# A transformer block on one core: spare products in the opening, codes before background, and a root moved to GpSimd

## The chip, the cores and the metric

One core of a Trainium2 chip runs the whole program in one launch. The metric is the time of one execution in device microseconds, as the median of several runs. Shorter is better. "TensorE" is the matrix engine (PE in the profile), "VectorE" is DVE, "ScalarE" is ACT, "GpSimd" is POOL, and SyncE (SP) issues the DMAs.

## The reference

All inputs are bfloat16. The sequence has 2048 rows of 512 numbers.

```python
def _A_ref(x, wqkv, wo):                      # attention, 32 heads of 16
    qkv = ((x @ wqkv).reshape(B, S, 3, 32, 16)).transpose(2, 0, 3, 1, 4)
    q, k, v = qkv[0], qkv[1], qkv[2]
    scores = jnp.einsum("bhqd,bhkd->bhqk", q, k) * (16 ** -0.5)
    p = softmax(scores, axis=-1)
    o = jnp.einsum("bhqk,bhkd->bhqd", p, v)
    return o.transpose(0, 2, 1, 3).reshape(B, S, 512) @ wo

def _B_ref(x, w_gate, w_up, w_down):          # gated feed-forward, 1792 wide
    return (sigmoid(x @ w_gate) * (x @ w_up)) @ w_down

h  = x + _A_ref(layernorm(x), wqkv, wo)
h2 = h + _B_ref(layernorm(h), w_gate, w_up, w_down)
```

## The kernel before, in words

**Opening.** x is loaded in four chunks of 512 rows, transposed on TensorE and copied out. The first layer norm is folded into the projections: its mean is taken out of the weights, and its reciprocal deviation comes from products of x with itself (`gram`), `diagonal`, `variance`, `deviation` and `rstd0`. Keys and queries of the first four heads are built at once (`kproj0`, `queries0`, `turn_kq`). The order of these steps is not written by hand. Each is a `Task` with the engines it may run on and an assumed cost. While the program is built, a loop takes the task with the best key (start time less a share of its rank), and issues it. Products that start before the constant `COLD` are priced 1.9 times higher there. Two PSUM buffers named `g0` hold gram products, two named `h0` the key projections.

**Main stage.** The 32 heads form groups of four; a *group* of work is four heads with 512 queries, or eight heads with 256. A unit is one head strip, 128 keys and 512 score columns. 2048 units are cut into 683 *score tiles* of three. TensorE writes a tile to `pss` (L1024); two such tiles exist. ScalarE takes the exponential of all three units (128x1536) or of two (128x1024, L1375) into one of six buffers `pt`. In the second case VectorE takes the third unit: it writes a bfloat16 bit pattern that approximates the exponential (a *first code*, `J`, L1189), and when up to four first codes are together, three shifted copies of them (*codes*, L1209, kept as a `Chain`). The products of all four patterns with V are added up. TensorE's products with V go to one accumulator `acc` (L1163). When the last product of a group is in, `finish_group` transposes and normalizes it (L1105); only then may the next group's products with V begin.

Between these, TensorE works off a queue of *background*: the projections of later heads, then for each 256 rows the output projection, the second layer norm, and the feed-forward. Background is a queue of generators (`bg`); `credit` grows with every exponential and is spent by background products.

**What sets the order.** While the program is built, a planner keeps one clock per engine (`T`) and lets the engine that is furthest behind take its next step: `pe_step`, `act_step` or `dve_step`. Jobs for VectorE wait in `dq` and for ScalarE in `aq`, each with an assumed duration. `dve_step` takes the first codes before the jobs, and the jobs before the `Chain` of further codes. The engines then run the resulting queues strictly in order. `fill` adds a product without use where the planner finds TensorE too little used.

**The second layer norm.** For each of seven blocks of 256 rows, `wo_add` takes the statistics on VectorE (L162), and `newton_jobs` computes 1/sqrt(variance + 1e-5) for two columns by a bit trick and two Newton steps (L800 to L811). Two scalings (L855) need the result, then come transposes on TensorE and the feed-forward. The last block of 256 rows is done after the last exponential, by ScalarE's square root.

Of the kernel before, what the change touches and what calls it, by code (L numbers as in the profile page):

```python
# [26 lines left out]
def kernel(  # L27
# [11 lines left out]
    nc = tc.nc  # L39
    P = 128  # L40
    S, D = A_x.shape[1], A_x.shape[2]
# [9 lines left out]
    TQ = QC // P  # L51
# [55 lines left out]
    meanw = prep.tile([P, P], BF16)  # L107
# [108 lines left out]
        return ps0.tile([P, 512], FP32, name="b0")[:]  # L216

    nc.scalar.activation(out=small.tile([P, 1], FP32, name="warm")[:], in_=eps_t[:], func=ACT.Sqrt)

    kfull = small.tile([P, 1], FP32, name="kfull", bufs=1)  # L220
    buf = {}
# [221 lines left out]

    CHUNK_FIRST = (5300, 1700, -1300, 600)
    KIND_FIRST = {'g': -300, 'rc': 500, 'qm': 500, 'h': -700, 't': -700, 'rr': -2000, 'kr': 2000, 'qr': -3000, 'e': -5000, 'va': 5000, 'ke': -6000, 'va0': -6000, 'kk': -6000, 'kt': -7000}
    COLD = 7000.0
    RANKED = 0.032

    free = {"P": 0.0, "A": 2500.0, "D": 3300.0, "G": 8000.0}
    banks, grams, projs = 4, 2, 2  # L450
    left = {n for n, t in tasks.items() if t.end is None}
    while left:
        best = None
        for n in left:
            t = tasks[n]
            ends = [tasks[d].end for d in t.deps]
            if None in ends or t.bank > banks or t.gram > grams or t.proj > projs:
                continue
            at = max(ends, default=0.0) + 90
            if n == "go":  # L460
                t.end = at
                continue
            kind = n[0] if isinstance(n, tuple) else n
            rk = rank_of(n) + KIND_FIRST.get(kind, 0) + (
                CHUNK_FIRST[n[1]] if isinstance(n, tuple) else 0)
            for eng, ns, fn in t.opts:
# [12 lines left out]
        grams -= t.gram  # L479
        projs -= t.proj  # L480
        left.discard(n)
        fn()
# [14 lines left out]

    LAT = 100.0
    T = {e: max(0.0, free[e] - tasks["go"].end) for e in "PAD"}
    SPQ, LAND = 630.0, 2000.0  # L500
    sp = {"t": 0.0}

# [42 lines left out]
        def end(self):  # L545
            return None if self.job.end is None else self.job.end + self.ns

    dq, aq, chains = [], [], []
    prior = {"op": None}
    BUBBLE = 119  # L550
    class State(dict):
# [2 lines left out]
            if key == "pm":  # L554
                super().__setitem__("open", False)

    st = State(**{"n": 0, "open": False, "cur": 0, "pm": None, "mark": None, "acc": None, "mode": "b", "work": "b", "ot": 0})

    def dve(ns, fn, *deps):
        dq.append(Job(ns, fn, deps))  # L560
        return dq[-1]

    def act(ns, fn, *deps):
        aq.append(Job(ns, fn, deps))
        return aq[-1]

    class Chain:
        def __init__(self, ops, after):
            self.ops, self.after = deque(ops), after

        def left(self):
            return sum(o[0] for o in self.ops)
# [5 lines left out]
    def pending():  # L578
        return sum(c.left() for c in chains)
# [3 lines left out]

    def pop_chain():
        c = next_chain()
        T["D"] += c.cost()
        _, _, f = c.ops.popleft()
        c.after.append(object())
        prior["op"] = c.after[-1]
        f()  # L590
        if not c.ops:
            chains.remove(c)

    def flush():
        moved = True
        while moved and (dq or aq):
            moved = False
            for q, e in ((dq, "D"), (aq, "A")):
# [193 lines left out]
    def newton_jobs(dst, var, *deps):  # L792
        n = var.shape[1]
        v = small.tile([P, n], FP32, name="nv")
        y = small.tile([P, n], FP32, name="ny")
        t = small.tile([P, n], FP32, name="nt")
        V = nc.vector

        def seed():
            V.tensor_scalar(out=v[:], in0=var, scalar1=1e-5, scalar2=None, op0=ALU.add)  # L800
            V.tensor_scalar(out=t[:].bitcast(I32), in0=v[:].bitcast(I32), scalar1=1,
                            scalar2=None, op0=ALU.logical_shift_right)
            V.tensor_scalar(out=y[:].bitcast(I32), in0=t[:].bitcast(I32), scalar1=-1.0,
                            scalar2=float(0x5F3759DF), op0=ALU.mult, op1=ALU.add)

        def step(out):
            V.tensor_tensor(out=t[:], in0=y[:], in1=y[:], op=ALU.mult)
            V.tensor_tensor(out=t[:], in0=t[:], in1=v[:], op=ALU.mult)
            V.tensor_scalar(out=t[:], in0=t[:], scalar1=-0.5, scalar2=1.5,
                            op0=ALU.mult, op1=ALU.add)  # L810
            V.tensor_tensor(out=out, in0=y[:], in1=t[:], op=ALU.mult)  # L811
# [315 lines left out]
    def av_cost(uns):  # L1127
        return MM * max(sum(un.u[3] == j for un in uns) for j in range(4))
# [70 lines left out]
    def dexp_rest():  # L1199
        J, uns = half[0], half[1:]  # L1200
        half.clear()
        k = len(uns)
        j = J[:, 0:k, :]
        mine = first_codes[-1]
        mine[0] += NCODE - 1

        def code(i):
            c = dvx.tile([P, NJ, QC], U16, name="code", bufs=CB)[:, 0:k, :]
            nc.vector.tensor_scalar(out=c, in0=j, scalar1=CODE_STEP[i], scalar2=None, op0=ALU.add)  # L1209
# [7 lines left out]
        chains.append(Chain([(75 + 134 * k, 0, lambda i=i: code(i)) for i in range(NCODE)], [J]))  # L1217

    def drop_read():
        for c in (codes, first_codes):  # L1220
# [58 lines left out]
    def pe_step():  # L1279
# [109 lines left out]
    def dve_step():  # L1389
        t = T["D"]  # L1390
        job = next((j for j in dq if j.ready() is not None and j.ready() <= t), None)
        if job and jq and t - sc_end[jq[0][0]] < 400:
            dq.remove(job)
            job.place("D")
            return
        drop_read()
        if jq and sc_end[jq[0][0]] + LAT <= t + WAITJ and (half or len(first_codes) < NJB):
            n, pss, un, ex = jq.popleft()
            first = dexp_first(pss, un)
            T["D"] = max(t, sc_end[n] + LAT) + 600  # L1400
            ex_end[n] = max(un.end, T["D"])
            tc.declare_no_dep(first.ins, ex.ins, reason="other banks of the tile")
            readers[n] = (ex, first)
            return
        for job in dq:
            r = job.ready()
            if r is not None and r <= t + 60:
                dq.remove(job)
                job.place("D")
                return  # L1410
        if chains:
            pop_chain()
            return
        T["D"] = t + 40
# [19 lines left out]
            wd = load_wd()  # L1434
            load_xr(0)

    steps = {"P": pe_step, "A": act_step, "D": dve_step}
    while nxt["e"] < N or jq:
        e = nxt["e"]
        if e == N:  # L1440
            dve_step()
            continue
        steps[min("PAD", key=lambda k: T[k])]()
        if nxt["e"] > e:
            after_exp(e)
    if half:
# [107 lines left out]
```

## Time and profile before

| | before |
|---|---|
| time, median of 3 runs | 827.53 us (825.93 to 829.72) |
| the profiled execution | 828.4 us, of which the span from first to last instruction is 826.6 us |
| mean granted clock of TensorE | 0.979 |
| busy: TensorE, VectorE, ScalarE, GpSimd | 763.5, 738.2, 770.3, 8.4 us |
| first exponential starts, last one ends | 22.8 us, 794.4 us |

How to read the rows: a row of groups ends in "busy, mean ns of one | idle time of the engine just before, and what ended most of it". A row of the timeline has start, duration, engine, line, operation, output and inputs, and in brackets the idle time before it and what ended it. A row of windows has the stretch and its length, the busy time of each engine with its number of instructions, the clock granted to TensorE (1.00 is full), the share of the DMA engines, and GB/s. A row of waits has the total in us, the number of waits, and the longest.

### The profile page before, as it was taken

To read this page: it belongs to the slowest core of one execution; us is meant where nothing else is said; L and a number is where in the kernel's file an instruction comes from. 1 tells how busy PE (TensorE), PEld (TensorE's weight loads), DVE (VectorE), ACT (ScalarE), POOL (GpSimd) and SP (SyncE) were. 2 spreads that over 40 slices of the span, in tenths; PEclk is the share of its full clock that TensorE was granted. 3 is DMA by queue.
4 is the path that set the end of the run, shared out by engine and by line. 5 is a ranking of instruction groups with operands and counts; after the bars stand their busy time and mean duration, and the time that the engine had idled before them with its cause. 6 is when DMAs were issued, how large, how long until landed. Compare 5 with 4: busy or idle time off the path is not lost.

```text
span 826.6 us, 34438 instructions
## 1 busy us (share of the span) xinstructions
PE 763.5 (92%) x15176; PEld 371.3 (45%) x15179; DVE 738.2 (89%) x1410; ACT 770.3 (93%) x780; POOL 8.4 (1%) x30
## 2 busy tenths in 40 slices
PE   7899999888888998999998999999999999999998
PEld 6322222333333534455544443555454445545556
DVE  7799899999979898999999889899989998989962
ACT  6898999999998999899999998999999999999962
POOL 3000000000000000000000000000000000000000
PEclk9698999999989999999999999999999999999999
DMA  6402012122400223013101230231032202332500
GB/s 188 116 2 62 7 27 60 28 60 60 130 5 22 60 62 93 10 48 105 54 16 53 68 110 13 68 85 54 21 94 59 73 16 67 103 95 78 166 26 18
DMA packets 91860, 51.30 MB, mean 62 GB/s; under 512 B 21376, under 2 KB 90624, under 8 KB 91712
## 3 DMA queue, kind: packets, MB, share of 16 engines
q1 hardware_dynamic: 91184, 49.03, 21.5%
q8 instruction: 120, 1.97, 1.0%
q14 instruction: 28, 0.23, 0.1%
q10 hardware_dynamic: 528, 0.07, 0.1%
HBM read 39.52 MB, written 2.11 MB: 50 GB/s over the span
## 4 chain that ended last, share of the span: by engine, by line
PE 38%; ACT 37%; issue 13%; DVE 10%; DMA 1%; SPq 0%; ACTq 0%; DVEq 0%
ACT pt L1375 35%; PE pm L186 11%; PE acc L1163 11%; PE pss L1024 10%; DVE J L1189 4%; DVE code L1209 2%; PE gu L181 1%; ACT th L894 1%; DVE xs L1105 1%; DMA RQ<-rows 1%; PE hp L1519 1%; PE b L177 1%; PE g L249 1%; DVE hT L878 0%; PE pm L626 0%
## 5 line engine op out<-in xcount | busy, mean ns | idle before, releaser
L1375 ACT ACTIVATE pt<-pss 128x1024 bf16<-128x1024 f32 (+1 forms) x683 | 729.5, 1188 | 24.3 <-PE pss L1024 11.7
L1189 DVE TENSOR_SCALAR J<-pss 128x512 uint16<-128x512 f32 x480 | 320.0, 681 | 27.1 <-PE pss L1024 25.1
L1024 PE MATMUL pss<-QT,KT 32*128 32x256 bf16 (+1 forms) x3584 | 272.9, 292 | 44.6 <-ACT pt L1375 29.8
L1209 DVE TENSOR_SCALAR code<-J 128x2048 uint16<-128x2048 uint16 (+3 forms) x387 | 238.7, 645 | 0.2
L1163 PE MATMUL acc<-pt,Vaug 128*17 128x256 bf16 (+1 forms) x2742 | 222.8, 293 | 2.2 <-DVE xs L1105 1.2
L1024 PEld LDWEIGHTS <-KT 32*128 32x128 bf16 x3584 | 83.7, 92 | 249.9 <-ACT pt L1375 136.0
L1163 PE MATMUL acc<-code,Vaug 128*17 128x256 bf16 (+1 forms) x2526 | 187.7, 290 | 0.0
L1163 PEld LDWEIGHTS <-Vaug 128*17 128x17 bf16 x6110 | 137.6, 90 | 96.5 <-issue 77.0
L1163 PE MATMUL acc<-J,Vaug 128*17 128x256 bf16 (+1 forms) x842 | 136.9, 295 | 0.0
L186 PE MATMUL pm<-xT,wgu 128*32 128x256 bf16 x3136 | 117.2, 274 | 1.7 <-DVE hT L878 0.9
L186 PEld LDWEIGHTS <-wgu 128*32 128x32 bf16 x3136 | 76.7, 96 | 28.3 <-issue 25.1
L186 PE MATMUL pm<-wd,hT 128*32 128x512 bf16 x784 | 54.7, 382 | 0.4 <-DVE h L843 0.4
L878 DVE SCALAR_TENSOR_TENSOR hT<-th,pm 128x512 bf16<-128x512 f32 x49 | 33.3, 680 | 10.3 <-PE pm L186 9.3
L894 ACT ACTIVATE th<-pm 128x512 f32<-128x512 f32 x49 | 30.8, 629 | 0.8 <-PE pm L186 0.2
L1105 DVE STREAM_TRANSPOSE xs<-acc 128x512 f32<-128x512 f32 x32 | 22.8, 711 | 9.2 <-PE acc L1163 8.2
L186 PEld LDWEIGHTS <-hT 128*32 128x32 bf16 x784 | 16.1, 95 | 20.2 <-issue 12.6
L186 PE MATMUL pm<-xT,wk_sb 128*32 128x512 bf16 x256 | 19.3, 383 | 1.1 <-DVE kd L668 0.8
L186 PE MATMUL pm<-xT,wq_sb 128*32 128x512 bf16 x256 | 19.1, 382 | 0.1
L186 PE MATMUL pm<-wv_sb,xT 128*32 128x448 bf16 x256 | 17.6, 370 | 0.5 <-DVE Vaug L206 0.4
L186 PE MATMUL pm<-wo_sb,ot 128*32 128x512 bf16 x224 | 17.3, 397 | 0.7 <-DVE hT L878 0.5
L888 DVE SCALAR_TENSOR_TENSOR ob<-pm,h 128x512 bf16<-128x512 f32 x14 | 9.6, 684 | 4.9 <-PE pm L186 4.9
L1083 DVE STREAM_TRANSPOSE ot<-o 128x256 bf16<-128x256 bf16 x32 | 13.5, 432 | 0.1
(152 smaller groups left out, 344.5 us busy)
## 6 DMA issues: line engine op xcount, KB each, us to landing
wgu<-in_B_w_gate_dram SPq DMA_DIRECT2D x49, 256.0 KB
wgu<-in_B_w_up_dram SPq DMA_DIRECT2D x49, 256.0 KB
KT<-ones SPq DMA_DIRECT2D x7, 512.0 KB
out_dram<-ob SPq DMA_DIRECT2D x15, 128.0 KB
KT<-kd SPq DMA_DIRECT2D x28, 64.0 KB
QT<-qd SPq DMA_DIRECT2D x112, 16.0 KB
wd<-in_B_w_down_dram SPq DMA_DIRECT2D x1, 1792.0 KB
xr<-in_A_x_dram SPq DMA_DIRECT2D x14, 128.0 KB
```

The source lines that it names most:

```text
L177: nc.tensor.transpose(out=pt[:, b, :], in_=part, identity=ident_bf[:])
L186: nc.tensor.matmul(ps[r, :], lhsT=lhsT[:, r], rhs=rhs, start=start, stop=stop, tile_position=(0, 32 * j), skip_group_check=True)
L878: nc.vector.scalar_tensor_tensor(out=hT[:, 2 * k:2 * k + 2, :].rearrange("p f q -> p (f q)"), in0=th[:], scalar=1.0, in1=ps, op0=ALU.add, ...
L888: nc.vector.scalar_tensor_tensor(out=ob[:], in0=ps, scalar=0.5, in1=fstate.pop((h, i))[:], op0=ALU.mult, op1=ALU.add)
L894: nc.scalar.activation(out=th[:], in_=ps, func=ACT.Tanh, scale=0.5)
L1024: mm = nc.tensor.matmul(pss[:, ui, a * w:(a + 1) * w], lhsT=KT[hg[a]][32 * j:32 * j + 32, kt * P:(kt + 1) * P], rhs=(QT0[q] if q < NQC and ...
L1083: nc.vector.transpose(out=ot[:], in_=o2[:, i * NB:(i + 1) * NB, :] .rearrange("p b r -> p (b r)"))
L1105: j = st["acc"] = dve(630, lambda: nc.vector.transpose(out=xs[:].rearrange("p b r -> p (b r)"), in_=acc[:]), Mark(T["P"]))
L1163: nc.tensor.matmul(acc[32 * j:32 * j + VW, a * w:(a + 1) * w], lhsT=Vaug[:, kt, 4 * hg[a] + j, :], rhs=un.ap[:, a * w:(a + 1) * w], start= ...
L1189: first = nc.vector.tensor_scalar(out=J[:, k, :], in0=src, scalar1=128 * SC * LOG2E, scalar2=float(CODE_BASE), op0=ALU.mult, op1=ALU.add)
L1209: nc.vector.tensor_scalar(out=c, in0=j, scalar1=CODE_STEP[i], scalar2=None, op0=ALU.add)
L1375: ex = nc.scalar.activation(out=pt[:, lo:lo + wa, :], in_=pss[:, lo:lo + wa, :], func=ACT.Exp, scale=SC)
```

## The change

1. **Spare products in the opening.** 18 products of `meanw` with itself are issued at the start into a buffer `h0`. In the opening's loop, a new helper `idle` issues up to 8 products of 512 columns into a buffer `g0` where the loop sees TensorE wait; it does so in one place, between the second and the third transposition of keys. `COLD` goes from 7000 to 4500.
2. **Codes of a closed group first.** A `Chain` now knows its group. `dve_step` takes a code before the waiting jobs when the group that TensorE is closing lies more than 3 tiles back.
3. **Reciprocal root on GpSimd.** `newton_jobs` issues to GpSimd. The seed takes two instructions for three. GpSimd gets a queue `gq`, a step `gps_step` and a clock of its own in the planner. A lock between GpSimd and the chains (`lock`, `unlocked`) exists in the planner, but no job sets it.
4. **Background ahead.** When no first code waits and VectorE's clock with all its pending codes is less than 300 ns ahead of TensorE's, background may be issued with `credit` down to -4 (the third condition, fewer than 100 tiles to the group's end, always holds: a group has some 21 tiles).

```diff
+    spare = ps0h.tile([P, TQ, P], FP32, name="h0")[:]
+    for _ in range(18):
+        nc.tensor.matmul(spare[:, 0, :], lhsT=meanw[:], rhs=meanw[:], start=True, stop=True)
...
-    COLD = 7000.0
+    COLD = 4500.0
...
+    def idle(n):
+        if n > 0 and "idle" not in buf:
+            buf["idle"] = ps0g.tile([P, TQ, P], FP32, name="g0")[:]
+        for _ in range(min(n, 8)):
+            E.matmul(buf["idle"], lhsT=xT[3][:, 0, 0, :], rhs=xT[3][:, 0, :, :], start=True, stop=True)
...
         t = tasks[n]
+        if eng == "P" and free["P"] > 9000.0:
+            idle(int((start - free["P"] - 200.0) // 216))
         free[eng] = t.end = start + ns
...
+    def gps_step():
+        t = T["G"]
+        for job in gq:
+            r = job.ready()
+            if r is not None and r <= t + 60:
+                gq.remove(job)
+                job.place("G")
+                if job.lock:
+                    st["lock"] = T["G"] - job.ns, T["G"]
+                return
+        T["G"] = t + 40
...
-        V = nc.vector
+        V = nc.gpsimd
 
         def seed():
             V.tensor_scalar(out=v[:], in0=var, scalar1=1e-5, scalar2=None, op0=ALU.add)
-            V.tensor_scalar(out=t[:].bitcast(I32), in0=v[:].bitcast(I32), scalar1=1,
-                            scalar2=None, op0=ALU.logical_shift_right)
-            V.tensor_scalar(out=y[:].bitcast(I32), in0=t[:].bitcast(I32), scalar1=-1.0,
+            V.tensor_scalar(out=y[:].bitcast(I32), in0=v[:].bitcast(I32), scalar1=-0.5,
                             scalar2=float(0x5F3759DF), op0=ALU.mult, op1=ALU.add)
...
-        j = dve(600, seed, *deps)
-        j = dve(800, lambda: step(y[:]), j)
-        return dve(800, lambda: step(dst), j)
+        j = gps(1100, seed, *deps)
+        j = gps(1050, lambda: step(y[:]), j)
+        return gps(1050, lambda: step(dst), j)
...
+    HURRY = -3
...
+        group = tiles[min(e, N - 1)][-1][:2]
+        floor = -4 if not jq and T["D"] + pending() < t + 300 and lasts[group] - e < 100 else 0
         order = []
-        if st["work"] == "b" and st["mode"] != "s" and credit > 0 and not (press and pick):
+        if st["work"] == "b" and st["mode"] != "s" and credit > floor and not (press and pick):
             order.append("b")
         if last or press or good and credit < 2:
             order.append("a")
-        if credit > 0:
+        if credit > floor:
             order.append("b")
...
+        if chains and chains[0].group == gseq[st["cur"]] and lasts[chains[0].group] < nxt["e"] + HURRY:
+            pop_chain()
+            return
         for job in dq:
...
-    steps = {"P": pe_step, "A": act_step, "D": dve_step}
+    steps = {"P": pe_step, "A": act_step, "D": dve_step, "G": gps_step}
```

More of the change, by code (lines that the diff above doesn't have):

```diff
@@ L499 @@
     T = {e: max(0.0, free[e] - tasks["go"].end) for e in "PAD"}
+    T["G"] = 0.0
     SPQ, LAND = 630.0, 2000.0
@@ L546, in end @@
             return None if self.job.end is None else self.job.end + self.ns
-    dq, aq, chains = [], [], []
+    dq, aq, gq, chains = [], [], [], []
     prior = {"op": None}
@@ L555, in __setitem__ @@
                 super().__setitem__("open", False)
-    st = State(**{"n": 0, "open": False, "cur": 0, "pm": None, "mark": None, "acc": None, "mode": "b", "work": "b", "ot": 0})
+    st = State(**{"n": 0, "open": False, "cur": 0, "pm": None, "mark": None, "acc": None, "mode": "b", "work": "b", "ot": 0, "lock": (0.0, 0.0)})
     def dve(ns, fn, *deps):
@@ L565, in act, with gps, unlocked, __init__ @@
         return aq[-1]
+    def gps(ns, fn, *deps, lock=False):
+        gq.append(Job(ns, fn, deps))
+        gq[-1].lock = lock
+        return gq[-1]
+    def gps_step():
[9 more added lines that the diff above has]
+        T["G"] = t + 40
+    def unlocked(t):
+        return st["lock"][1] if st["lock"][0] <= t < st["lock"][1] else t
     class Chain:
-        def __init__(self, ops, after):
-            self.ops, self.after = deque(ops), after
+        def __init__(self, ops, after, group):
+            self.ops, self.after, self.group = deque(ops), after, group
         def left(self):
@@ L585, in pop_chain @@
         c = next_chain()
-        T["D"] += c.cost()
+        T["D"] = unlocked(T["D"]) + c.cost()
         _, _, f = c.ops.popleft()
@@ L595, in flush @@
         moved = True
-        while moved and (dq or aq):
+        while moved and (dq or aq or gq):
             moved = False
-            for q, e in ((dq, "D"), (aq, "A")):
+            for q, e in ((dq, "D"), (aq, "A"), (gq, "G")):
                 for job in list(q):
@@ L808, in step @@
             V.tensor_tensor(out=t[:], in0=t[:], in1=v[:], op=ALU.mult)
-            V.tensor_scalar(out=t[:], in0=t[:], scalar1=-0.5, scalar2=1.5,
-                            op0=ALU.mult, op1=ALU.add)
+            V.tensor_scalar(out=t[:], in0=t[:], scalar1=-0.5, scalar2=1.5, op0=ALU.mult, op1=ALU.add)
             V.tensor_tensor(out=out, in0=y[:], in1=t[:], op=ALU.mult)
-        j = dve(600, seed, *deps)
-        j = dve(800, lambda: step(y[:]), j)
-        return dve(800, lambda: step(dst), j)
+        j = gps(1100, seed, *deps)
+        j = gps(1050, lambda: step(y[:]), j)
+        return gps(1050, lambda: step(dst), j)
     out_v = out[0].rearrange("(t p) d -> p t d", p=P)
@@ L1216, in code @@
                 due[un.u[0], un.u[1], un.u[3]] -= i == NCODE - 1
-        chains.append(Chain([(75 + 134 * k, 0, lambda i=i: code(i)) for i in range(NCODE)], [J]))
+        chains.append(Chain([(75 + 134 * k, 0, lambda i=i: code(i)) for i in range(NCODE)], [J], uns[0].u[:2]))
     def drop_read():
@@ L1442 @@
             continue
-        steps[min("PAD", key=lambda k: T[k])]()
+        steps[min("PADG", key=lambda k: T[k])]()
         if nxt["e"] > e:
```

## The prediction

> **What bounds the kernel now.** I read the page first: three engines lie close together, so no share of busy time says who leads.
>
> ```profile
> PE 763.5 (92%) x15176; PEld 371.3 (45%) x15179; DVE 738.2 (89%) x1410; ACT 770.3 (93%) x780; POOL 8.4 (1%) x30
> ```
>
> Next the windows view, cut where the exponentials begin and end, and the waits and groups of their line (L1375).
>
> ```profile
> 22.84:794.42 771.58, 718.74 (x14665) 338.46 (x14668) 709.15 (x1332) 747.06 (x732) 0.30 (x1) 0.98 0.22 60
> ACT pt L1375 <- PE pss L1024: 11.7, 24, 1.0
> ACT pt L1375 <- PE acc L1163: 9.5, 4, 3.3
> L1375 ACT ACTIVATE pt<-pss 128x1024 bf16<-128x1024 f32 x481 | 469.8, 1063 | 22.6 <-PE pss L1024 11.0 <-PE acc L1163 9.5
> L1375 ACT ACTIVATE pt<-pss 128x1536 bf16<-128x1536 f32 x202 | 289.2, 1488 | 1.7 <-PE pss L1024 0.7 <-ACT pt L1375 0.3
> ```
>
> In the 771.6 us of the main stage ScalarE works 747.1 and stands still 24.5. So the time is: opening (22.8), plus ScalarE's work, plus its 24.5 us of gaps, plus the end (826.6 - 794.4 = 32.2). In the built programs the instruction order from the last score tiles to the end is the same on TensorE, ScalarE and VectorE; I take the end as unchanged. What can move is the opening, the work, and the gaps. The timeline of ScalarE names the gaps. The four long ones, each at the close of a group of heads:
>
> ```profile
> 82.15 2.37 ACT L1375 ACTIVATE pt<-pss 128x1024 bf16<-128x1024 f32 x2 [2.81 <-PE acc L1163]
> 269.89 2.85 ACT L1375 ACTIVATE pt<-pss 128x1024 bf16<-128x1024 f32 x3 [3.32 <-PE acc L1163]
> 343.59 21.43 ACT L1375 ACTIVATE pt<-pss 128x1024 bf16<-128x1024 f32 x20 [2.45 <-PE acc L1163]
> 438.94 3.71 ACT L1375 ACTIVATE pt<-pss 128x1024 bf16<-128x1024 f32 x3 [0.88 <-PE acc L1163]
> ...
> 736.87 19.78 ACT L1375 ACTIVATE pt<-pss 128x1536 bf16<-128x1536 f32 x18
> ```
>
> They make 2.81 + 3.32 + 2.45 + 0.88 = 9.46 us. (The last row, with no gap before or in it, is used below.) The second place is the first exponentials, where the granted clock (the column behind the products' count) has fallen to half:
>
> ```profile
> 25.63 2.85 ACT L1375 ACTIVATE pt<-pss 128x1024 bf16<-128x1024 f32 x3 [0.85 <-PE pss L1024]
> 28.90 1.02 ACT L1375 ACTIVATE pt<-pss 128x1024 bf16<-128x1024 f32 x1 [0.41 <-PE pss L1024]
> 30.89 1.02 ACT L1375 ACTIVATE pt<-pss 128x1024 bf16<-128x1024 f32 x1 [0.97 <-PE pss L1024]
> 32.40 1.02 ACT L1375 ACTIVATE pt<-pss 128x1024 bf16<-128x1024 f32 x1 [0.48 <-PE pss L1024]
> 33.65 7.80 ACT L1375 ACTIVATE pt<-pss 128x1536 bf16<-128x1536 f32 x7 [0.23 <-PE pss L1024]
> ...
> 19.00:20.00 1.00, 0.63 (x5) 0.71 0.03 8
> 20.00:21.00 1.00, 1.00 (x8) 0.50 0.00 0
> ...
> 33.00:34.00 1.00, 1.00 (x14) 0.96 0.47 105
> ```
>
> From the shares 0.71 and 0.96 the clock fell at 19.4 and rose at 33.1: 13.7 us at half speed, with 0.85 + 0.41 + 0.97 + 0.48 + 0.23 = 2.94 us of ScalarE's gaps. The rest of the 24.5 is small, or lies in later spells at half clock.
>
> **The opening.** In before, the first product waits for x at 3.05; four products take 0.61 us until 9 us, then 0.39:
>
> ```profile
> 0.83 0.17 DVE L132 MEMSET meanw<- 128x128 bf16 x1 [0.83 <-PEq L1538]
> 3.05 1.31 PE L177 MATMUL b<-ident_bf,code 128*128 128x128 bf16 x8 [3.05 <-DMA code<-in_A_x_dram]
> 6.67 0.61 PE L249 MATMUL g<-xT 128*128 128x128 bf16 x4
> 9.45 0.39 PE L249 MATMUL g<-xT 128*128 128x128 bf16 x4
> 6.00:7.00 1.00, 1.00 (x14) 1.00 1.01 175
> 10.00:11.00 1.00, 1.00 (x26) 1.00 0.93 300
> 19.37 0.56 PE L333 MATMUL b<-ident_bf,code 128*128 128x128 bf16 x4 [1.91 <-DVE rstd L281]
> 798.09 1.46 PE L1472 MATMUL hp<-wo_sb,ot 128*128 128x512 bf16 x6
> ```
>
> TensorE starts 14 products in the seventh microsecond and 26 in the eleventh (the column's 1.00 notwithstanding). The 18 spare products need only meanw, ready at 1.0. At 14 per us they end by 2.3, and even if they are slower the wait for x until 3.05 covers nearly all. TensorE is then busy 2 us sooner; if it speeds up 2 us sooner, 2 us of slow work shrink to 1. Bounds: +0.2 (x is late anyway and the products overhang) to -1.9; I take -1.0, between the two. The short chain from 19.4 to the first scores (transposes and the maximum product, 0.56 per four against 0.39) would run at full clock: two such steps lie on the path, -0.3. The new list order swaps a few neighbours only, and its DMAs stay in their order.
>
> The 8 products of 512 columns go ahead of the transposes that wait 1.91 us in before. Six such products take 1.46 us, so about (1.46 - 0.38) / 5 = 0.22 each beyond the first, 1.7 us for eight: the wait covers them, and without that cover they would cost 1.7. If they keep the clock up, most of the 2.94 us goes; VectorE's work and the score round trip keep some: -2.5. By the Trainium skill, "TensorE: Matmul & The Clock Gate", Part 1, the clock falls only after an idle window of about 3.4 us. This trace disagrees in part: the longest gap in the rows around 19 us is 1.91, and the clock fell. By that rule the gap was no cause, and the gain would be 0 instead of 2.5. I follow the trace: sparse work was enough, so denser work should help, but the phase of such a window is open.
>
> **ScalarE's work.** The built order has 487 narrow and 196 wide exponentials for 481 and 202. Six units move to VectorE: 6 x (1488 - 1063) ns = -2.55 us. The price is on VectorE:
>
> ```profile
> L1189 DVE TENSOR_SCALAR J<-pss 128x512 uint16<-128x512 f32 x480 | 320.0, 681 | 27.1 <-PE pss L1024 25.1
> L1209 DVE TENSOR_SCALAR code<-J 128x2048 uint16<-128x2048 uint16 x333 | 218.4, 682 | 0.1
> 262.40 0.16 DVE L800 TENSOR_SCALAR nv<-mv 128x2 f32<-128x2 f32 x1
> 265.32 0.16 DVE L811 TENSOR_TENSOR rstd<-ny,nt 128x2 f32<-128x2 f32 x1
> L809 DVE TENSOR_SCALAR nt<-nt 128x2 f32<-128x2 f32 x14 | 2.4, 170 | 0.5
> L808 DVE TENSOR_TENSOR nt<-nt,nv 128x2 f32<-128x2 f32 x14 | 2.2, 160 | 0.5
> ```
>
> 6 x 0.68 = 4.1 for the first codes; the further codes stay 387, of which nine of the shortest become longer, under 9 x 0.68 = 6.1. Off VectorE go 77 small root instructions, about 0.16 each and 0.03 between: 15 us. Net at least -4.8, so that queue gets shorter, not longer.
>
> **The closes.** When a group ends, its last codes must be multiplied before the next group's products may start; meanwhile the six buffers of exponentials fill, and ScalarE stops. I counted, in TensorE's built order, how many score tiles stand behind a group's last one before the group is closed. In before the four stalled groups have 6, 7, 7 and 6; one group has 5, and it closes within the row of 18 exponentials without a gap from 736.87 to 756.65. After: 5, 3, 4 and 2. Three groups rise to 5 from 2 or 3. So three stalls should go (3.32 + 2.45 + 0.88 = 6.65), the first shrink by an exponential (1.06), and three new places may cost up to the 2.81 - 1.06 = 1.75 that would be left of the first, each. Bounds -7.7 to -2.5; since the one known five costs nothing, 0.5 each: -6.2. This is what the closed group's codes, and the root off VectorE, do together: at 262.40 to 265.48 the root stood in that queue just ahead of the 3.32 us gap. Background ahead by up to four products is part of the same order and gets no sum of its own; without room it isn't issued.
>
> **The root on GpSimd.** Ten instructions in a row, 7 times. The nearest rows are two that hang on each other:
>
> ```profile
> 10.72 0.20 POOL L309 TENSOR_TENSOR r<-rstd 128x4 f32<-128x4 f32 x1 [3.73 <-DVE rstd L281]
> 11.00 0.22 POOL L310 TENSOR_TENSOR kk<-kk,r 128x16 f32<-128x16 f32 x1
> 261.31 0.17 DVE L162 BATCH_NORM_AGGREGATE mv<-st 128x2 f32<-128x6 f32 x1
> 266.00 1.00 DVE L855 TENSOR_SCALAR xT<-h,mv,rstd 128x512 bf16<-128x512 f32 x2
> ```
>
> 0.28 from start to start, so 2.8 us. In before 4.7 us lie between the statistics and the scaling that waits for the root. In the built order VectorE has six to eight instructions of other work there in six cases, at 0.24 to 0.71 each 4.0 to 4.7 us, and three (2.0 us) in one: on average 4.0. So it is hidden but for 0.8 us, unless the two engines hinder each other: behind the waiting scaling on VectorE stand the first codes, and for these waits the score tile. No row shows a GpSimd instruction beside a code of 0.68 us. The Trainium skill, "GPSIMD Engine Reference", Specifications, has GpSimd share its SBUF interface with VectorE's two-port modes; no run so far shows it. My bounds come from rows: below, -1 (a shorter VectorE queue); above, GpSimd held for each code in the stretch (one to five, 0.68 each), which overruns the other work by 2.2, 2.1 and three times under 0.9, about 6, and the 70 instructions each holding a code 0.2 us in the 3 cases of 10 in which one runs, 4. The likely value is nearer the uncontended rows: +2.
>
> **Sum.** -1.0 - 0.3 - 2.5 - 2.55 - 6.2 + 2.0 = -10.55 against the profiled execution's 828.4 (span 826.6 and 1.8 around it): 817.9. That execution lay 0.9 above the median of 827.53, so 817.0 for the median.
>
> **Rivals.** *The clock falls anyway.* After the eight products some 2.5 us of short transposes and waits follow, hardly denser than what let it fall. For it: the fall with a gap of 1.91 alone. The Trainium skill, "TensorE: Matmul & The Clock Gate", Part 4, adds that transposes don't count as a busy TensorE in the same way; no row here separates them. Then 2.5 + 0.3 are lost: 819.8. Chance 0.25.
>
> *The stall moves on.* Codes put first make the background wait, and the closes come back as waits for projections, or three new fives cost their full 1.75. Against it: the counts above. Then the closes bring about nothing: 817 + 6.2, with 2 us more for late background: 825. Chance 0.17.
>
> *GpSimd sets the pace (slower).* If a root instruction takes much longer beside VectorE's codes than 0.28, the scaling stands at the head of VectorE's queue, and ScalarE soon runs out of score tiles. The cover is 4.0 us, so it shows from 0.40 per instruction. The other terms gain 12.55, 1.8 for each of the seven roots: from (4.0 + 1.8) / 10 = 0.58 there is nothing left. At 0.65 each root stalls 2.5, together 17.5: 828.4 - 12.55 + 17.5 - 0.9 = 832.5. For it: no row beside codes; against it: 0.20 and 0.22 beside other VectorE work. Chance 0.13.
>
> The forecast keeps 0.45. Range: all lower bounds together, -1.9 - 0.3 - 2.9 - 2.55 - 7.7 - 1 = -16.4, give 811 for the median; upward it takes in both middle cases, and the later of them with half of the root's bound of +8 over the value taken. So 811 to 829, which leaves out the slower case and a little below 811. A measurement here tells some 0.5% (4.1 us) from no change. Below 823.4 lie the forecast and the fallen clock: 0.70; within: 0.17; slower: 0.13.
>
> **What would show it.** Right: the granted clock is 1.0 from about 7 us on and through 20 to 33; first exponentials near 21.5; 487 and 196 exponentials; ScalarE's wait for acc falls from 9.5 to about 3; GpSimd's starts lie 0.28 apart and the scaling (L855 in before) doesn't wait for it. Wrong: 0.50 stays in the windows from 20 on; acc still holds ScalarE 8 us or more; VectorE shows waits for GpSimd of over a microsecond at seven places.

## The result, and the profile after

| | median of runs | against the kernel before, 95% interval |
|---|---|---|
| before | 826.73 us (4 runs, 824.07 to 829.72) | |
| after | 818.47 us (4 runs, 816.49 to 819.09) | 0.9873 [0.9836, 0.9909] |
| after, measured again on another chip | 818.8 us (6 runs; before 829.3) | 0.9877 [0.9847, 0.9908] |

The change makes the kernel 1.3% faster: 817.0 was forecast, 818.5 measured. The profiled execution of after took 819.09 us with a span of 817.3, at a mean granted clock of 0.987 (before 0.979). First the engines on its page, then its windows row for the main stage, cut as in the prediction.

```profile
PE 761.1 (93%) x15237; PEld 368.0 (45%) x15241; DVE 731.9 (90%) x1339; ACT 768.9 (94%) x780; POOL 27.8 (3%) x100
```

```profile
21.47:785.11 763.64, 714.72 (x14701) 334.93 (x14704) 702.71 (x1261) 745.88 (x732) 19.72 (x71) 0.99 0.23 61
```

The first exponential starts at 21.47 us, 1.37 earlier than before. The main stage has 763.64 us, 7.94 fewer: ScalarE's work fell from 747.06 to 745.88 (-1.2), and its gaps from 24.52 to 763.64 - 745.88 = 17.76 (-6.8). These sizes hold for one execution of each kernel: a second profile of the changed program (`after_again`, below) starts at 21.45 us and has 746.02 us of work, but gaps of 22.35. The end is 817.3 - 785.1 = 32.2, as before. VectorE has 71 instructions fewer (70 went to GpSimd, seven went altogether, six first codes came).

The groups of the exponentials (now L1408) and two kinds of waits in after; the scaling is now L885, first codes are L1220 and codes L1240:

```profile
L1408 ACT ACTIVATE pt<-pss 128x1024 bf16<-128x1024 f32 x487 | 473.7, 1055 | 12.1 <-PE pss L1054 8.4 <-PE acc L1194 1.1
L1408 ACT ACTIVATE pt<-pss 128x1536 bf16<-128x1536 f32 x196 | 279.4, 1477 | 5.6 <-PE pss L1054 4.6 <-PE acc L1194 0.2
```

```profile
ACT pt L1408 <- PE pss L1054: 13.0, 25, 1.2
ACT pt L1408 <- PE acc L1194: 1.2, 2, 1.1
DVE xT L885 <- POOL rstd L841: 1.2, 1, 1.2
```

ScalarE's waits for a group's close (acc) fell from 9.5 us in four to 1.2 in two; those for score tiles (pss) rose from 11.7 to 13.0 (17.9 in the second profile). The scaling waited for GpSimd once, for 1.2 us. In the timeline of ScalarE, the gaps between 22 and 34 us are gone; others at half clock stand later:

```profile
21.47 15.14 ACT L1408 ACTIVATE pt<-pss 128x1024 bf16<-128x1024 f32 x15 [0.51 <-PE pss L1054]
...
120.69 4.26 ACT L1408 ACTIVATE pt<-pss 128x1024 bf16<-128x1024 f32 x4 [1.07 <-PE acc L1194]
125.72 1.45 ACT L1408 ACTIVATE pt<-pss 128x1536 bf16<-128x1536 f32 x1 [0.76 <-PE pss L1054]
128.00 1.02 ACT L1408 ACTIVATE pt<-pss 128x1024 bf16<-128x1024 f32 x1 [0.83 <-PE pss L1054]
130.26 1.02 ACT L1408 ACTIVATE pt<-pss 128x1024 bf16<-128x1024 f32 x1 [1.24 <-PE pss L1054]
```

The windows of after show that TensorE starts 26 products in the eighth microsecond (14 in before), and they show the clock (the column behind the engines' counts): 1.00 in the 21st microsecond, where before had 0.50. Later it falls to half five times (four times in before, besides the opening). One of these falls lies inside a gap of TensorE, whose row of the timeline follows: the share of 0.62 puts it at 124.2 us.

```profile
7.00:8.00 1.00, 1.00 (x26) 1.00 (x24) 0.96 (x3) 0.74 (x2) 0.00 (x0) 1.00 1.02 295
20.00:21.00 1.00, 0.33 (x5) 0.17 (x4) 0.78 (x2) 0.80 (x2) 0.00 (x0) 1.00 0.04 8
124.00:125.00 1.00, 0.00 (x0) 0.00 (x0) 1.00 (x2) 0.95 (x1) 0.00 (x0) 0.62 0.13 31
126.00:127.00 1.00, 1.00 (x15) 0.25 (x7) 0.00 (x0) 1.00 (x1) 0.00 (x0) 0.50 0.05 12
```

```profile
125.00 0.61 PE L1054 MATMUL pss<-QT,KT 32*128 32x512 bf16 x3 [1.93 <-ACT pt L1408]
```

Last, one of the seven roots on GpSimd and VectorE's rows beside it, from the timeline:

```profile
341.15 0.17 DVE L162 BATCH_NORM_AGGREGATE mv<-st 128x2 f32<-128x6 f32 x1
341.24 2.47 DVE L1240 TENSOR_SCALAR code<-J 128x2048 uint16<-128x2048 uint16 x4
341.42 1.13 POOL L833 TENSOR_SCALAR nv<-mv 128x2 f32<-128x2 f32 x1 [82.91 <-DVE mv L162]
342.63 0.53 POOL L834 TENSOR_SCALAR ny<-nv 128x2 int32<-128x2 int32 x1
343.24 0.52 POOL L838 TENSOR_TENSOR nt<-ny 128x2 f32<-128x2 f32 x1
343.63 0.68 DVE L1220 TENSOR_SCALAR J<-pss 128x512 uint16<-128x512 f32 x1
343.84 0.20 POOL L839 TENSOR_TENSOR nt<-nt,nv 128x2 f32<-128x2 f32 x1
344.12 0.19 POOL L840 TENSOR_SCALAR nt<-nt 128x2 f32<-128x2 f32 x1
344.23 0.68 DVE L1240 TENSOR_SCALAR code<-J 128x2048 uint16<-128x2048 uint16 x1
344.40 0.56 POOL L841 TENSOR_TENSOR ny<-ny,nt 128x2 f32<-128x2 f32 x1
...
345.88 0.20 POOL L841 TENSOR_TENSOR rstd<-ny,nt 128x2 f32<-128x2 f32 x1
346.11 1.00 DVE L885 TENSOR_SCALAR xT<-h,mv,rstd 128x512 bf16<-128x512 f32 x2 [1.20 <-POOL rstd L841]
```

Beside a first code an instruction takes 0.20 us and the next starts 0.28 later (343.84 to 344.12); the last four, while VectorE waits, take as long. Beside four codes of VectorE the first took 1.13 us, the next two 0.53, and one beside a single code 0.56. Every stretched instruction of the seven chains overlaps a code. This chain took 4.7 us, the longest of the seven; their mean is 3.5.

### The profile page after: what moved, and what is told of

It reads as the page before. It is cut to its first block, busy times and chain, and to the rows that moved or that the text cites. A ratio compares the mean times of both kernels' runs of the same rounds, so it can differ in the third digit from the quotient of the medians.

```text
span 817.3 us, 34573 instructions
## 1 busy us (share of the span) xinstructions
PE 761.1 (93%) x15237; PEld 368.0 (45%) x15241; DVE 731.9 (90%) x1339; ACT 768.9 (94%) x780; POOL 27.8 (3%) x100
## 4 chain that ended last, share of the span: by engine, by line
PE 46%; ACT 33%; issue 11%; DVE 8%; DMA 2%; SPq 1%; ACTq 0%; DVEq 0%
ACT pt L1408 31%; PE pm L186 15%; PE acc L1194 13%; PE pss L1054 13%; DVE J L1220 3%; PE gu L181 2%; DMA RQ<-rows 1%; DVE xs L1136 1%; DVE code L1240 1%; ACT th L924 1%; PE hp L1555 1%; DVE hT L908 1%; DMA code<-in_A_x_dram 1%; DMA wgu<-in_B_w_gate_dram 0%; DVE ot L1114 0%
## 5 line engine op out<-in xcount | busy, mean ns | idle before, releaser
L1408 ACT ACTIVATE pt<-pss 128x1024 bf16<-128x1024 f32 (+1 forms) x683 | 727.9, 1176 | 17.8 <-PE pss L1054 13.0
L1220 DVE TENSOR_SCALAR J<-pss 128x512 uint16<-128x512 f32 x486 | 322.2, 681 | 23.9 <-PE pss L1054 22.2
L1240 DVE TENSOR_SCALAR code<-J 128x2048 uint16<-128x2048 uint16 (+3 forms) x387 | 239.9, 651 | 0.2
L1194 PE MATMUL acc<-pt,Vaug 128*17 128x256 bf16 (+1 forms) x2731 | 220.3, 293 | 1.8 <-DVE Vaug L206 0.9
L1194 PE MATMUL acc<-code,Vaug 128*17 128x256 bf16 (+1 forms) x2559 | 184.1, 290 | 1.9 <-DVE code L1240 1.9
L1194 PE MATMUL acc<-J,Vaug 128*17 128x256 bf16 (+1 forms) x853 | 134.2, 292 | 0.3 <-DVE xs L1136 0.3
L186 PE MATMUL pm<-xT,wgu 128*32 128x256 bf16 x3136 | 115.3, 274 | 2.5 <-DVE hT L908 2.3
L186 PEld LDWEIGHTS <-hT 128*32 128x32 bf16 x784 | 16.3, 95 | 18.6 <-issue 11.2
L833 POOL TENSOR_SCALAR nv<-mv 128x2 f32<-128x2 f32 x7 | 3.9, 561 | 534.6 <-DVE mv L162 534.6
L186 PE MATMUL pm<-xT,wk_sb 128*32 128x512 bf16 x256 | 19.3, 383 | 0.5 <-DVE kd L701 0.5
```

What stands on the lines that cost most here:

```text
L186: nc.tensor.matmul(ps[r, :], lhsT=lhsT[:, r], rhs=rhs, start=start, stop=stop, tile_position=(0, 32 * j), skip_group_check=True)
L1194: nc.tensor.matmul(acc[32 * j:32 * j + VW, a * w:(a + 1) * w], lhsT=Vaug[:, kt, 4 * hg[a] + j, :], rhs=un.ap[:, a * w:(a + 1) * w], start= ...
L1220: first = nc.vector.tensor_scalar(out=J[:, k, :], in0=src, scalar1=128 * SC * LOG2E, scalar2=float(CODE_BASE), op0=ALU.mult, op1=ALU.add)
L1408: ex = nc.scalar.activation(out=pt[:, lo:lo + wa, :], in_=pss[:, lo:lo + wa, :], func=ACT.Exp, scale=SC)
```

## The experiments

Each version was run in five rounds beside the kernel before. The expectations on record name their theories by letters. In short, A first has each part bring something of its own; from `root_open` on it says that the opening and the root are the whole gain. B has the opening and its clock bring nearly everything (from `root_open` on: the clock evens the gains out), C the root's move, and D has the codes' rule and the early background count, with or without the root. What E to H and B' say belongs to one kernel each. All results at a glance:

| version | median, us (before, same chip) | ratio, 95% interval | mean clock of its runs |
|---|---|---|---|
| `open`: before + opening | 826.88 (828.91) | 0.9965 [0.9947, 0.9983] | 0.985 |
| `root`: before + root on GpSimd | 818.10 (828.91) | 0.9857 [0.9830, 0.9884] | 0.990 |
| `hurry`: before + codes of a closed group first | 828.11 (828.91) | 0.9990 [0.9967, 1.0014] | 0.983 |
| `floor`: before + background ahead | 825.73 (828.91) | 0.9949 [0.9924, 0.9973] | 0.983 |
| `root_open`: root + opening | 815.02 (829.35) | 0.9837 [0.9809, 0.9864] | 0.994 |
| `no_root`: the change, root on VectorE | 825.98 (829.35) | 0.9960 [0.9938, 0.9983] | 0.987 |
| `no_hurry`: the change, codes not first | 822.82 (829.35) | 0.9917 [0.9884, 0.9949] | 0.988 |
| `root_on_vector`: `root`'s order, VectorE's work | 822.78 (829.35) | 0.9937 [0.9919, 0.9956] | 0.989 |
| `after_again`: the change | 818.80 (829.30) | 0.9877 [0.9847, 0.9908] | 0.988 |
| `long_root`: the change, root of 18 instructions | 834.15 (829.30) | 1.0062 [1.0041, 1.0084] | 0.979 |
| `start18`: before + 18 spare products | 829.12 (829.30) | 0.9993 [0.9974, 1.0011] | 0.982 |
| `idle8`: before + 8 products of 512 columns | 827.03 (829.30) | 0.9977 [0.9956, 0.9998] | 0.986 |

The kernel before ran 76 times beside these, at a mean clock of 0.981.

### The parts alone

`open` has part 1 of the change alone (`spare`, `idle`, `COLD`).

> The opening's part alone in the kernel before: 18 spare products, the 8 products ahead of the third transposition of keys, and the price limit of 4500. The main stage's built order is that of before (same exponentials, same closes at 6, 7, 7, 6 tiles). Theory A (three separate gains: opening, closes, narrower exponentials): first exponential about 1.4 us sooner, the 2.9 us of gaps at half clock gone, ScalarE's wait for acc still about 9.5: 4 us faster, ratio about 0.995. Rival B (the opening and the clock are the whole gain; gaps in the main stage only change places): ratio about 0.988. Rival C (moving the root is the whole gain of the main stage; the codes' rule and the early background bring nothing): same as A here.

0.9965, near A: the opening brings 0.35%, 2.9 us, not the whole. In its profile ScalarE still waits 9.9 us for closes (9.5 in before).

`root` has part 3 alone: the queue `gq`, `gps_step`, and

```diff
-        V = nc.vector
+        V = nc.gpsimd
...
-        j = dve(600, seed, *deps)
-        j = dve(800, lambda: step(y[:]), j)
-        return dve(800, lambda: step(dst), j)
+        j = gps(1100, seed, *deps)
+        j = gps(1050, lambda: step(y[:]), j)
+        return gps(1050, lambda: step(dst), j)
```

> The root on GpSimd alone, in the kernel before. The built order has 490 first codes (10 units more off ScalarE) and only two closes over 4 tiles, both at 6. Theory A: 10 x 0.425 = 4.3 less exponential work, acc waits from 9.5 to about 4, opening as before: 7 us faster, ratio 0.9915. Rival B: ratio 1.000. Rival C: all that the main stage gained in the full change or more, ratio 0.990.

0.9857, more than any theory gave it: by itself this part brings as much as the whole change. Its windows row, its narrow exponentials and its waits:

```profile
21.97:784.71 762.74, 713.20 (x14720) 336.66 (x14722) 706.55 (x1261) 743.49 (x732) 22.48 (x71) 0.99 0.23 61
```

```profile
L1393 ACT ACTIVATE pt<-pss 128x1024 bf16<-128x1024 f32 x491 | 478.8, 1055 | 16.8 <-PE pss L1042 10.0 <-PE acc L1181 4.8
```

```profile
ACT pt L1393 <- PE pss L1042: 11.3, 22, 2.5
ACT pt L1393 <- PE acc L1181: 4.8, 2, 2.8
```

ScalarE works 743.5 us in it, 3.6 less than in before (491 narrow exponentials for 481), and its gaps are 762.74 - 743.49 = 19.3 for 24.5. VectorE waits for GpSimd once in this profile, for 0.2 us.

`hurry` has part 2 alone.

```diff
+        if chains and chains[0].group == gseq[st["cur"]] and lasts[chains[0].group] < nxt["e"] + HURRY:
+            pop_chain()
+            return
         for job in dq:
```

> The rule that puts a closed group's codes ahead of VectorE's jobs, alone, in the kernel before. The built order has 477 first codes (3 units more on ScalarE, +1.3 us) and closes at 5, 5, 5, 5, 7 and 7. Theory A: two stalls at 7 remain (about 2.5 each), acc waits fall from 9.5 to about 6: 2 us faster, ratio 0.998. Rivals B and C: ratio 1.000 to 1.002.

0.9990, no difference that the runs can tell. Its waits:

```profile
ACT pt L1376 <- PE pss L1024: 14.9, 26, 1.9
ACT pt L1376 <- PE acc L1164: 1.4, 2, 1.1
```

The closes did what the prediction said of them: 9.5 us fell to 1.4. But the waits for score tiles rose from 11.7 to 14.9, and ScalarE's work in the main stage from 747.1 to 749.1 us, since three first codes fewer are made. So of 8.1 us some 5 came back in this profile, and its main stage is 1.4 us shorter than that of before. That the stall moved on fits this; but two profiles of the changed program differ by 4.9 us in their waits for score tiles, so one profile doesn't show it.

`floor` has part 4 alone.

```diff
+        floor = -4 if not jq and T["D"] + pending() < t + 300 and lasts[group] - e < 100 else 0
...
-        if credit > 0:
+        if credit > floor:
```

> Background issued up to four products ahead, alone, in the kernel before. The built order has 481 first codes and closes at 6, 5, 7, 6, 5. Theory A: the close that fell from 7 to 5 loses its 3.3 us, the others stay: 3 us faster, ratio 0.996. Rivals B and C: ratio 1.000.

0.9949, near A's 0.996: 4.2 us of 829 from the part to which the prediction gave no sum of its own.

### Two parts, and one part left out

`root_open` has parts 1 and 3, `no_root` parts 1, 2 and 4, `no_hurry` parts 1, 3 and 4.

> The root on GpSimd and the opening's part together, without the codes' rule and the early background. Main stage in the order of the root alone (490 first codes, closes at 6 and 6), opening in the order of the opening alone. If the two gains are separate (theory A now: opening, and the root as the whole of the main stage's gain), their ratios multiply: 0.9857 x 0.9965 = 0.982, 14 us faster than before, and faster than the full change. Rival B (the clock evens it out: a spell at half clock removed in the opening comes back later): 0.986, as the root alone. Rival D (the codes' rule and the early background are needed beside the opening): 0.988 or above.

> The full change with the root back on VectorE (opening, codes' rule, early background). 475 first codes: 11 units fewer on VectorE than in the full change, 4.7 us more exponential work; seven closes at 5, none above. Theory A now (the root is the main stage's gain): ratio 0.996, the opening alone. Rival D (closes at 5 or less are what counts, by whatever means): acc waits under 2 us, so 6 to 8 us come off the gaps, less 2 us of work added against before: ratio 0.990.

> The full change without the rule that puts a closed group's codes first. 485 first codes, closes at 6, 7 and 5. Theory A now: the rule brings nothing once the root is off VectorE: as the full change, ratio 0.987, or better. Rival D: the two closes at 6 and 7 bring back 2 to 3 us each: ratio 0.993.

Without the root the change is worth 0.9960, what the opening alone is worth: parts 2 and 4 bring nothing on top, as A had it. With the root and the opening alone it is 0.9837; the interval holds both A's 0.982 and B's 0.986. Adding background ahead makes that worse: 0.9917, and the two intervals don't overlap. Here A missed with 0.987, and D had 0.993. Their waits, first of `root_open`, then of `no_hurry`:

```profile
ACT pt L1405 <- PE pss L1054: 8.9, 21, 1.3
ACT pt L1405 <- PE acc L1193: 4.8, 2, 2.8
```

```profile
ACT pt L1407 <- PE pss L1054: 11.4, 21, 2.3
ACT pt L1407 <- PE acc L1193: 5.8, 4, 2.8
```

In these two profiles 3.5 us of the 4.8 by which the main stages differ are in these waits; five units went back to ScalarE besides. The rule that gained 0.5% where VectorE had the root costs 0.8% where it hasn't. That background issued early takes VectorE's turn from first codes fits this, but no run shows it apart. With codes first it is 0.9877; the intervals overlap, so it isn't settled that this wins a part back.

### What the root's gain consists of

`root_on_vector` keeps the planner's order of `root`, and issues the same 70 instructions to VectorE instead.

```diff
-        V = nc.gpsimd
+        V = nc.vector
```

> The root alone, planned as on GpSimd (same built order of all else: 490 first codes, closes at 6 and 6), but its 70 instructions issued to VectorE at the places the planner gave them. Theory E (the gain lies in the order that the freed VectorE time allows, which needs that time): VectorE gets 70 x 0.19 = 13 us back, in seven pieces of 1.9 us ahead of first codes; part is taken up by its own waits, so 5 to 8 us of the root's 11.8 are lost: ratio 0.992 to 0.995. Rival F (the planner's different order alone is the gain, VectorE had the room): ratio 0.986 as with the root on GpSimd.

0.9937, as E had it. Of the 1.43% of `root`, 0.63% come with the order (the planner, which thinks VectorE freer, makes ten more first codes and closes groups sooner) and with the seven instructions that the shorter seed saves. The other 0.80%, 6.6 us, need VectorE to be free of the 70. In the waits, first of `root`, then of `root_on_vector`, TensorE is held longer by first codes:

```profile
PE pss L1042 <- DVE J L1207: 5.9, 18, 1.1
PE pss L1042 <- DVE J L1207: 10.5, 28, 1.1
```

How this reaches ScalarE isn't shown: its own waits for score tiles are 11.3 us in both profiles, and its gaps 19.3 and 21.6.

`long_root` asks what the wait for GpSimd costs when it comes. It adds two Newton steps, eight instructions, to each root of the full change; the planner's assumed costs stay, and so the order.

```diff
-        j = gps(1050, lambda: step(y[:]), j)
+        j = gps(1050, lambda: (step(y[:]), step(y[:]), step(y[:])), j)
```

> The full change with two Newton steps more on GpSimd (18 instructions in a row for 10; the planner's costs and the whole built order of the other engines are unchanged; the result only gets more exact). By the uncontended rows each root takes 8 x 0.28 = 2.2 us more, 5.7 for the 3.5 that the profile of the full change shows on average. Theory G (cover is 4.0 us, as in the prediction): VectorE's scalings wait 1.7 us at each of seven places, 12 in all, of which ScalarE feels about half: 6 us slower than the full change, ratio 0.995. Rival H (the cover is much longer than counted, since VectorE itself waits for score tiles there): scaling waits under 4 us in all, ratio within 0.002 of the full change.

1.0062, 15.4 us slower than the change as it is (1.0062 - 0.9877 = 0.0185 of 829), where G gave half of the wait and H nothing. The waits, and one of the seven places in the timeline:

```profile
DVE xT L885 <- POOL rstd L841: 13.8, 7, 3.4
ACT pt L1408 <- PE pss L1054: 27.2, 46, 2.4
```

```profile
350.03 1.00 DVE L885 TENSOR_SCALAR xT<-h,mv,rstd 128x512 bf16<-128x512 f32 x2 [3.42 <-POOL rstd L841]
...
351.78 0.40 PE L1054 MATMUL pss<-QT,KT 32*128 32x256 bf16 x6 [2.30 <-DVE J L1220]
```

The scaling stands at the head of VectorE's queue, the first code behind it, TensorE's next score tile behind that, and ScalarE's waits for score tiles rise by 27.2 - 13.0 = 14.2 us. Against the second profile of the change, with 17.9 us of these waits, they rise by 9.3. So two thirds or all of the 13.8 us come through, and the time rose by 15.4. The chains took 5.9 us on average, so the other work covered 5.9 - 13.8 / 7 = 3.9 of each.

### The opening's two halves

`start18` adds the 18 spare products to before and nothing else, `idle8` the 8 products of 512 columns.

> Only the 18 spare products at the start, in the kernel before (price limit 7000 as before, same main order). Theory A: full speed by about 5 to 7 us for 9, first exponential 1 us sooner; half clock from about 19 to 33 stays: ratio 0.9985. Rival B' (a warm start also keeps the clock up later): ratio 0.9965, as the whole opening part.

> Only the 8 products of 512 columns ahead of the third transposition of keys, in the kernel before. Theory A: no half clock between 19 and 33, 2.5 us of gaps gone: ratio 0.997. Rival B' (the short products behind still let the clock fall, or it falls later instead): ratio 1.000.

`start18` gives 0.9993, no effect that the runs can tell: the interval goes from 2.2 us faster to 0.9 slower, and A's 0.9985 lies in it. In its windows TensorE starts 22 products in the eighth microsecond and only 6 in the eleventh, where before had 26; its timeline has the reason:

```profile
7.00:8.00 1.00, 1.00 (x22) 1.00 0.92 301
10.00:11.00 1.00, 0.26 (x6) 1.00 1.04 331
```

```profile
11.07 0.40 PE L177 MATMUL b<-ident_bf,code 128*128 128x128 bf16 x4 [0.80 <-DMA code<-in_A_x_dram]
```

The spare products run at 10 to 11 a microsecond and end before x arrives; TensorE does speed up sooner, and then waits for x. `idle8` gives 0.9977, 1.9 us, near A's 0.997. The granted clock of the same stretch (18 to 36 us) in the windows of before, `start18` and `idle8`, in fences of their own:

```profile
18.00:36.00 18.00, 14.92 (x119) 0.62 0.54 133
```

```profile
18.00:36.00 18.00, 14.74 (x133) 0.72 0.53 133
```

```profile
18.00:36.00 18.00, 14.96 (x169) 1.00 0.53 133
```

In all eight profiles with the 8 products the clock in this stretch is 1.00; in all six without them it is between 0.62 and 0.91. So these products, and not the earlier start, keep it up. `COLD` was tested in `open` only, beside the products.

### The change again

`after_again` is the changed kernel without an edit, on the chip of the last three.

> The full change once more, beside the others on one chip. Theory A now: opening and root are the gain, the codes' rule and the early background add nothing or take a little: ratio 0.986 to 0.989, not below the 0.9837 of root and opening alone. Rival D: ratio 0.984 or below.

0.9877, as A had it. It gave a second profile of the same program: 823.81 us at a clock of 0.980, for 819.09 at 0.987. Its main stage is 768.37 us long, 4.73 more than in the first, nearly all of it in the gaps (22.35 for 17.76):

```profile
ACT pt L1408 <- PE pss L1054: 17.9, 30, 2.9
```

Time goes with the clock from run to run of each kernel: a straight line through the runs gives 4.5 us less for each 0.01 of clock in the 76 runs of before, and 3.3 to 5.5 in the other kernels. By these lines, and as an estimate, at 0.987 before would take 826.7 us, `open` 825.8, `root` 819.8, `root_on_vector` 824.1, `root_open` 817.8, `long_root` 830.8, and the change 819.6 (10 runs). So of the change's 10.5 us some 7 are order and work at equal clock, and some 3.5 are clock; of `open`'s 2.9 us two thirds are clock. By the same lines `root` and `root_on_vector` lie 4.3 us apart, and `long_root` and the change 11.2. The lines are no experiment: no run sets the clock by itself.

## Why the prediction was right, and where its steps were not

**Sign and size.** Both right, and the single profiles agree with the sum by stage: the opening -1.4 (forecast -1.3), ScalarE's gaps -6.8 (forecast -2.5 - 6.2 + 2.0 = -6.7), ScalarE's work -1.2 (forecast -2.55), the end 0. In the second profile of the change the gaps fell by 2.2 us only, so the agreement of this stage is in part luck. And the runs show that the sum came out by terms that were given to the wrong parts.

**The clock in the opening.** Right in its mechanism. The granted clock is 1.00 through the stretch from 18 to 36 us, and the first exponential starts at 21.47 (21.5 was forecast). *The clock falls anyway* is refuted for this stretch by eight profiles of eight. The rule of the Trainium skill that was weighed ("TensorE: Matmul & The Clock Gate", Part 1), by which a gap of 1.91 us couldn't have let the clock fall, doesn't hold here: with it the products would gain nothing, and they keep the clock up each time. The size was 1.9 us (`idle8`, interval 0.2 to 3.6) for 2.5.

**The 18 spare products.** The term of -1.0 isn't borne out: `start18` gives 0.9993, some 0.6 us, with an interval that holds both nothing and the term. The case that the prediction named as its bound, x late anyway, is what the trace of `start18` shows. The whole opening brought 2.9 us instead of 3.8. That the first exponential of after came 1.37 us sooner in its profile is weak evidence: in the six profiles without the 8 products it lies between 21.97 and 22.95. But `idle8` has it at 22.27, and the seven profiles with the whole opening at 21.43 to 22.02, so the spare products or `COLD` may add something to the eight.

**ScalarE's work.** The count was right (487 and 196), the price 0.425 for a unit nearly so: between exponentials that follow each other without a gap, the starts lie 0.93 (narrow) and 1.335 us (wide) apart, 0.40 for a unit. What the term left out is that an exponential overlaps the tail of the one ahead by some 0.13 us (its mean of 1055 ns against 0.93 from start to start), and each small gap breaks this. Before has 46 such breaks between exponentials (over 60 ns), after 59. As an estimate from these numbers that gives 6 x 0.40 - 13 x 0.13 = 0.7 us, against 1.2 measured. `root` has 46 and ten units less: 10 x 0.40 = 4.0, against 3.6 measured. No run shows the breaks' cost apart.

**The closes.** The counting of score tiles behind a group's end was right: the long waits went, the new fives cost next to nothing, and acc fell by 8.2 us (forecast 6.2). The step that failed is that these waits were counted as time gained, and credited to the codes' rule. `hurry` takes 8.1 us of them away as well and gains 0.8 us, with an interval that holds nothing. In its profile some 5 us come back, at the score tiles and as work, so for the codes-first rule alone the rival *the stall moves on* fits best. `root_open`, with 4.8 us of acc left, has a better median than the change with 1.2.

**The root.** Charged with +2.0, it is where the gain is: 0.9857 by itself, and 0.9960 for the change without it. The prediction had the parts of the price nearly right. The cover was 4.0 us a root in the count and 3.9 in `long_root`; the rows lie 0.28 us apart where no code runs beside them, and 0.6 or even 1.2 beside codes; the wait came to 1.2 us in all. That VectorE's queue gets shorter was worked out too (-4.8 us), and the root off VectorE was named as a share of the closes' -6.2; but by itself it was priced at nothing, with -1 as a bound, since the sum counts only ScalarE's work and gaps. `root` and `root_on_vector` show that it is worth 6.6 us on top of the order (4.3 at equal clock, by the estimate above). What fits is that some 12 us of small instructions (77 of 0.16) in front of first codes make VectorE late for score tiles: TensorE waits 5.9 us for first codes without them and 10.5 with them.

**Background ahead.** It got no sum of its own. Alone it is worth 0.5%; with the root it costs.

**GpSimd sets the pace.** The mechanism is real: `long_root` has a stall behind each root, and two thirds or more of it comes through. It didn't decide here, since the seven chains had a mean of 3.5 us, under the cover. The Trainium skill ("GPSIMD Engine Reference", Specifications) has GpSimd share its SBUF interface with VectorE's two-port modes; the trace agrees, with 1.13 us beside four codes for an instruction of 0.20 and no stretch beside first codes, though no row says in which mode a code runs.

**A better version.** `root_open` has the best median, 815.02 us, and a ratio of 0.9837 [0.9809, 0.9864] for the change's 0.9877 [0.9847, 0.9908]. The intervals overlap, so its lead over the change isn't settled; its lead over before is. Left open is why background ahead and the root work against each other.

## What to carry to other kernels

Engines that lie within a few per cent of each other wait for each other in turn: small instructions taken off the one that comes second can gain time (6.6 us here), if they stand in a strictly ordered queue ahead of what the others wait for. A wait put into such a queue can come through in full, so count the cover in the built order, and keep the chain under it. Test the parts of a planned order one by one: gains of planner rules don't add up, and a total that comes out right doesn't show that its terms are.

## What the runs showed of the hardware that was not expected

- In all six profiles without the eight products TensorE's granted clock fell behind one gap of 1.9 us, with none longer since x arrived. The fall came 0.05 us after the gap's end in before (19.4 us), 0.8 in `start18` and 2.6 in `root_on_vector`. Eight products of 512 columns (some 1.7 us) in that place kept it at 1.00 in eight of eight. In after it fell again at 124.2 us, 1.2 us into a gap of 1.93.
- The 76 runs of before lie between 824.5 and 835.4 us, at mean granted clocks from 0.971 to 0.989; a straight line gives 4.5 us for 0.01. So a single profile can't tell 3 us: two of the same kernel took 819.09 and 823.81.
- GpSimd's instructions on 128x2 tiles take 0.20 us, close to VectorE's 0.16. Beside first codes, which read PSUM, they stay at 0.20; beside codes, which read SBUF, they take up to 1.13.
